# Where two weight matrices are split, and in which order the first tile is normalized, in a fused attention and MLP kernel

## The chip, the cores and the metric
The kernel runs on one core of a Trainium2 chip. The metric is the device time of one execution in microseconds, as the median of several runs. In this kernel TensorE (PE) does the matrix products, VectorE (DVE) and ScalarE (ACT) work on elements and can read the accumulation banks (PSUM), GpSimd (POOL) works on elements in on-chip memory (SBUF), and the queue of SyncE (SP) issues most of the transfers to and from device memory, ACT's queue the others.

## What is computed
With 2048 rows of 1024 elements, 32 heads of 32 and an MLP of width 3584, all in float32:

```
xn  = layernorm(x)
qkv = xn @ wqkv                                  # q, k, v for 32 heads
p   = softmax(q k^T / sqrt(32));  s = concat(p v) @ wo
h   = xn @ w1 + b1
y   = (h * tanh(softplus(h))) @ w2               # mish
out = x + s * silu(y)
```

## The kernel before
Products that need float32 accuracy are made from split operands. A float32 tensor becomes a high part, rounded to the matmul's reduced float32 type (F32R), and a low part, the remainder. Three matmuls (high by high, high by low, low by high; `THREE`) replace one. `copy` makes a high part on ACT, `low(eng, ...)` subtracts on the engine given. So each weight tile must be loaded, split by a copy and a subtract, and then used at once or stored split in device memory and loaded again later. The lists `w1s` and `w2s` hold 28 split tiles each; a W1 tile has 128 columns of W1 (1024x128), a W2 tile 128 rows of W2 (128x1024, in two halves of 512 columns).

The program has five parts.

1. **Prologue.** The first tiles of x (128 rows each) and the four V weight tiles are loaded. `ln_a` takes a tile's statistics (DVE), `ln_r` makes the reciprocal root (two activations), `ln_b` refines it (four 128x1 operations on DVE), `ln_x` normalizes (ACT, for the first two tiles one half on DVE), `ln_t` transposes (PE), and `ln_c` splits the transposed tile into `xc` (ACT copies, DVE subtracts). `v_split` splits a V weight tile `vw`; for the first tile both steps are on POOL, for the last the subtracts are.
2. **V.** Two passes (heads 0 to 15, then 16 to 31) over 16 row tiles. `v_group(i, t)` makes 24 matmuls for one tile; `evac` copies the bank to `vst` and stores it. Pass 0 also transposes the next tile inside each group. The loop index t of pass 0 runs two ahead of the tile that is multiplied. The split `xc` of the last three row chunks (512 rows each) is stored to `xs` by 12 moves, one an iteration from t = 8, two behind the loop. `w1_early` is one step of a pipeline over the first 16 W1 tiles (`W1_V`): store the tile two before, load this one, split the one before (POOL, `w1p` tiles, two buffers). It is called in the last four iterations of pass 0 and in every iteration of pass 1.
3. **QK.** 16 column tiles of the Q and K weights by four row chunks, 24 matmuls each (`qk_group`). `qk_split(f)` splits a weight tile into a buffer of the same two-buffer ring as `w1p`. The result is split into `qst` (two buffers) and stored by ACT's queue. Beside it, `presplit` takes the other 12 W1 tiles and all 28 W2 tiles, half a tile a job (load `praw`; two ticks later copy and subtract on POOL; at the next tick store `pw`), one job a group and two in some. From f = 12 on, head 0's scores are formed to find the maximum of each row (`s_mm`, DVE reductions); for each group of four row tiles, `m_tail` negates the maxima (r1), splits them into an `hl` buffer (r2, ACT and DVE), turns them by a small matmul `mtp` (r3, line 535) and writes them as two rows of the query stack (r4). The steps are placed by ticks of `later`; one tick is one `qk_group`.
4. **Attention and MLP together.** A planner (`Plan`) walks five streams with a cost for each operation and fixes the order on all engines when the program is built: scores for the maxima (`s`), transposed scores (`t`) with the exponentials `p` on ACT, the running sum `z` of the exponentials on POOL (one 128x2048 addition a key tile), products with V (`pv`), and the MLP's `h` and `y` for four row chunks. The MLP takes W1 tiles from `w1s` (ring `w1`, 2 buffers) and W2 halves from `w2s` (`w2_op`, ring `w2`, 5 buffers). `m_chain` is the same maximum chain for the later heads, with a ring `hl` of two.
5. **Output projection** and the final combination.

The lines that place the early W1 steps and the end of V:

```python
        if t > NT - 3:
            w1_early()
...
for t in range(NT):
    v_group(1, t)()
    w1_early()
    if t == 9:
        qk_load(0)
    if t == 12:
        qk_split(0)
        qk_load(1)
```

Of the kernel before, what the change touches and what calls it, by code (L numbers as in the profile page):

```python
# [9 lines left out]
F32 = mybir.dt.float32  # L10
# [15 lines left out]

W1_V = 16
NS = H * NT
# [185 lines left out]
def body(ctx: ExitStack, tc: tile.TileContext, x, wqkv, wo, w1, b1, w2, out):  # L214
# [30 lines left out]
    nc.vector.memset(ones, 1.0)  # L245
    ident = consts.tile([P, P], F32, name="ident")
    make_identity(nc, ident)

    ident_r = consts.tile([P, P], F32R, name="ident_r")
    nc.vector.tensor_copy(ident_r, ident)  # L250
    nc.scalar.preload_act_table_set("natural_log_exp_and_others")
# [18 lines left out]
    def copy(out_, in_, scale=1.0):  # L270
        nc.scalar.activation(out_, in_, AF.Copy, scale=scale)  # L271

    def move(out_, in_, eng=None):

        (eng or nc.sync).dma_start(out_.bitcast(F32), in_.bitcast(F32))

    def low(eng, out_, in_, high):

        eng.tensor_tensor(out_, in_, high.bitcast(F32), ALU.subtract)  # L279
# [17 lines left out]
    xc = [xc0] + [[big.tile([P, 2, HK, 512], F32R, name=f"xc{c}_{i}") for i in range(2)] for c in range(1, NC)]  # L297

    va = ExitStack()
    vp = pool(va, "vp", 2, side="right")  # L300
# [8 lines left out]

    def v_split(i, j, high, rest):  # L310
        raw = vraw.pop((i, j))
        vw[i, j] = w = vp.tile([P, 2, 2, 512], F32R, tag="w", name=f"vw{i}_{j}", bufs=5)
        for k in range(2):
            if high is nc.scalar:
                copy(w[:, 0, k], raw[:, k])
            else:
                high.tensor_copy(w[:, 0, k], raw[:, k])
            low(rest, w[:, 1, k], raw[:, k], w[:, 0, k])

# [72 lines left out]

    def ln_c(t):
        c, r = t // 4, slice(t % 4 * P, t % 4 * P + P)
        for g in range(2):
# [32 lines left out]

    ln_a(0)
# [12 lines left out]
    ln_x(1, True)  # L444
    ln_a(2)
    ln_r(2)
    xts[3] = x_load(3)
    for t in range(2, NT + 2):
        if t < NT:
            ln_b(t)  # L450
        evac = v_group(0, t - 2, 18 if t == 2 else 8, (lambda: ln_t(t - 1)) if t <= NT else None)
        if t <= NT:
            ln_c(t - 1)
        if t < NT:
            ln_x(t)
        for m in (4, 5, 6) if t == 2 else (t + 4,):
            if m < NT:
                xts[m] = x_load(m)
        if t == 2:
            ln_a(3)  # L460
        if t + 2 < NT:
            ln_a(t + 2)
        if t + 1 < NT:
            ln_r(t + 1)
        if t in (NT - 4, NT - 3):
            for j in range(2):
                v_load(1, 2 * (t - NT + 4) + j)
        if t == NT - 2:
            v_split(1, 0, nc.scalar, nc.vector)
        if t == NT + 1:  # L470
            for j in range(1, 4):
                v_split(1, j, nc.scalar, nc.vector)
        evac()
        if t > 7:
            c, k = t // 4 - 1, t % 4 * 2
            move(xs[c][:, :, k:k + 2], xc[c][k // HK][:, :, k % HK:k % HK + 2])
        if t > NT - 3:
            w1_early()
    for k in (4, 6):
        move(xs[NC - 1][:, :, k:k + 2], xc[NC - 1][1][:, :, k % HK:k % HK + 2])  # L480
    nc.sync.dma_start(bias1, b1.rearrange("(f p) -> p f", p=P))
# [41 lines left out]

    hls = [early.tile([P, P], F32R, name=f"hl{i}") for i in range(2)]
    for t in hls:
        nc.vector.memset(t.bitcast(F32), 0.0)

    nc.vector.memset(early.tile([P, 32], F32, name="pad2"), 0.0)
    vt = {}

    def parts(i, n):
        return hls[i][:, :2 * n].rearrange("p (a b) -> p a b", a=2)

    def turn(tp, i):
        nc.tensor.matmul(tp[:, :P], hls[i], ident_r, start=True, stop=True)

# [29 lines left out]
    def m_tail(h, g, mx):  # L566
        nm = early.tile([P, NT], F32, tag=f"nm{g % 2}", name=f"nm{h}_{g}")[:, :4]
        hl = parts(g % 2, 4)
        mt = sp.tile([8, P], F32R, tag="mt", name=f"mt{h}_{g}")

        def r1():
            nc.vector.tensor_reduce(nm, mx[:, :4], axis=AX.X, op=ALU.max, negate=True)

        def r2():
            copy(hl[:, 0], nm)
            low(nc.vector, hl[:, 1], nm, hl[:, 0])

        def r3():
            tp = ps1.tile([P, 512], F32, tag="ps", name=f"mtp{h}_{g}")
            turn(tp, g % 2)  # L580
# [12 lines left out]
    def load_w1(n):  # L593
# [78 lines left out]
    for name, n in (("b", 7), ("s", S_B), ("t", T_B), ("d", D_B), ("o", 1), ("p", PS), ("z", 1), ("e", 1), ("r", 1), ("on", 1),  # L672
                    ("act", ACTS), ("w1", 2), ("w2", W2S), ("xc0", 1), ("xc1", 1), ("v", 2), ("mx", 2), ("nm", 2), ("hl", 2),
                    ("mt", 1), ("h", 2)):
        plan.ring(name, n)
# [47 lines left out]
    def m_chain(h, first, n, maxes, tiles):  # L723
# [5 lines left out]
        def r2(at):  # L729
            tiles["hl"] = at["hl"]  # L730
            copy(parts(tiles["hl"], n)[:, 0], tiles["nm"])

        def r3(at):
            hl = parts(tiles["hl"], n)
            low(nc.vector if h == 0 else nc.gpsimd, hl[:, 1], tiles["nm"], hl[:, 0])

        def r4(at):
            tiles["tp"] = tp = bank(at, f"mtp{h}_{first}")
            turn(tp, tiles["hl"])

# [157 lines left out]

    acts, act_ops, w2t, w2_ops, w1_ops, xc_ops, ys_ops = {}, {}, {}, {}, {}, {}, {}
    tile_time = total / (NC * FT - 1.5)  # L900
# [6 lines left out]

    def w2_op(m, need=()):
        def emit(at):
            w2t[m] = mlp.tile([P, 2, 512], F32R, tag=f"w2{at['w2']}", name=f"w2_{m}")  # L910
            B, dh, j = m // (2 * YB), m // YB % 2, m % YB
            move(w2t[m], w2s[B * YB % FT + j][:, :, dh * 512:(dh + 1) * 512])
        w2_ops[m] = op("SP", 0.1, emit=emit, need=need, take=["w2"], bytes_=P * 1024 * 4)

# [38 lines left out]
    def mish(n, made, t):  # L953
# [54 lines left out]
        act_ops[n] = op("DVE", 0.69, need=[p5], emit=d7, give=[("d", t["own"]), ("b", t["own"]), "h"])  # L1008

    yacc = mlp.tile([P, 4, D], F32, name="yacc")  # L1010

    def y_stream():
        for m in range(W2S):
            w2_op(m, [m_there[0, 3]])
        for B in range(NC * FT // YB):
            c, b = divmod(B, FT // YB)
            done = []
            for dh in range(2):
                for s in range(4):
                    t = {}  # L1020
                    for j in range(YB):
                        n, m_ = YB * B + j, (B * 2 + dh) * YB + j
                        for i, (p, q) in enumerate(THREE):
# [5 lines left out]
                            g = dh * 4 + s + (3 * j + i + 1) / (3 * YB)  # L1029
                            give = (["w2"] if s == 3 and i == 2 else []) + (["act"] if s == 3 and dh and i == 2 else [])  # L1030
# [3 lines left out]
                            m = Op("PE", MM, key=tile_time * due, emit=mm,  # L1034
                                   need=[act_ops[n], w2_ops[m_]], take=["d", "b"] if j == 0 and i == 0 else [], give=give)
                            if j == 0 and i == 0:
# [246 lines left out]
```

## Time and profile before
| | |
|---|---|
| median of 3 runs | 3427.31 us (3425.34 to 3428.84) |
| the profiled execution's own time | 3423.3 us |
| span of its instructions | 3421.1 us |
| busy share of the span: PE, DVE, ACT, POOL | 99%, 68%, 57%, 72% |
| mean granted clock of PE | 0.999 |

The profile comes from one execution. Times are in microseconds from the start of its span. A row of the timeline gives start, duration, engine and line, operation, output<-input, count, and in brackets the idle time before it with what ended it. PE is the matmuls, PEld the weight loads, SPq and ACTq the issuing of transfers. Windows give busy time by engine (with instruction counts), PE's granted clock, the share of DMA time and GB/s. Matmuls overlap, so a busy PE says that it had work, not that it ran at its peak.

### The profile page before, as it was taken

How to read it: one execution, taken by the hardware profiler on the slowest of the kernel's cores; microseconds unless marked ns; L12 is line 12 of the kernel's file. 1: busy time of each engine (PE TensorE's matmuls, PEld its weight loads, DVE VectorE, ACT ScalarE, POOL GpSimd, SP SyncE). 2: the span in 40 equal slices, each digit the busy share in tenths (PEclk: the TensorE clock that was granted, in tenths of full speed). 3: DMA queues.
4: the chain of work that ended last, by engine and by line, in shares of the span. 5: the costliest groups of instructions: out<-in, count | busy, mean ns of one | idle time of the engine just before them, and what ended most of it. 6: DMA issues, size and time to landing. Idle time of an engine off the chain costs nothing.

```text
span 3421.1 us, 45658 instructions
## 1 busy us (share of the span) xinstructions
PE 3389.4 (99%) x17059; PEld 2492.7 (73%) x17059; DVE 2340.5 (68%) x3763; ACT 1942.2 (57%) x3086; POOL 2453.3 (72%) x752
## 2 busy tenths in 40 slices
PE   8999999999999999999999999999999999999999
PEld 7878877677777767777677777777777767777687
DVE  6211226877878777788878787878878788776533
ACT  5211112766666667666666676666666666666621
POOL 0444443988888888888888888888888888888700
PEclk9999999999999999999999999999999999999999
DMA  5989888433334354343434443333445443333482
GB/s 200 326 292 317 301 309 289 124 109 102 118 106 124 102 170 132 116 112 111 124 99 124 149 148 111 112 113 110 124 112 183 123 123 112 112 114 121 136 297 85
DMA packets 289184, 529.60 MB, mean 155 GB/s; under 512 B 88426, under 2 KB 134506, under 8 KB 265706
## 3 DMA queue, kind: packets, MB, share of 16 engines
q1 hardware_dynamic: 269108, 484.74, 46.0%
q10 hardware_dynamic: 19856, 41.95, 3.3%
q8 instruction: 135, 2.21, 0.3%
q14 instruction: 85, 0.70, 0.1%
HBM read 386.89 MB, written 138.67 MB: 154 GB/s over the span
## 4 chain that ended last, share of the span: by engine, by line
PE 87%; DMA 7%; POOL 3%; DVE 2%; SPq 1%; ACT 0%; issue 0%; POOLq 0%; ACTq 0%; DVEq 0%
PE y L1027 18%; PE h L938 17%; PE t L790 13%; PE pv L837 13%; PE s L707 13%; PE op L1124 5%; DMA w2s<-pw 3%; PE v L328 3%; PE qk L631 3%; DMA w1s<-pw 2%; POOL pw L279 1%; DMA w1e<-in_B_w_dram 1%; PE zp L863 1%; DVE mx L713 1%; POOL pw L619 1%; POOL w1p L279 0%
## 5 line engine op out<-in xcount | busy, mean ns | idle before, releaser
L819 POOL TENSOR_TENSOR z<-z,p 128x2048 f32<-128x2048 f32 x448 | 2066.5, 4613 | 192.1 <-ACT p L268 162.5
L268 ACT ACTIVATE p<-t,zero 128x512 f32<-128x512 f32 x2048 | 1384.4, 690 | 636.1 <-PE t L790 618.3
L713 DVE TENSOR_REDUCE mx<-s 128x1 f32<-128x512 f32 x1984 | 1329.6, 686 | 435.4 <-PE s L707 427.8
L1027 PE MATMUL y<-w,act 128*128 128x512 f32 x2688 | 937.4, 391 | 0.6 <-DVE yacc L1047 0.5
L790 PE MATMUL t<-qstack,kstack 128*128 128x512 f32 x2048 | 801.5, 393 | 0.3 <-ACT p L268 0.2
L707 PE MATMUL s<-kstack,qstack 128*128 128x512 f32 x1984 | 779.6, 394 | 3.9 <-DVE mx L713 3.4
L938 PE MATMUL h<-xr,w 128*128 128x512 f32 x2016 | 713.5, 391 | 2.1 <-DMA w<-w1s 2.1
L1027 PEld LDWEIGHTS y<-w,act 128*128 128x128 f32 x2688 | 502.9, 188 | 118.4 <-issue 8.4
L790 PEld LDWEIGHTS t<-qstack,kstack 128*128 128x128 f32 x2048 | 384.0, 188 | 109.0 <-issue 16.8
L707 PEld LDWEIGHTS s<-kstack,qstack 128*128 128x128 f32 x1984 | 371.3, 188 | 126.5 <-issue 24.3
L837 PE MATMUL pv<-p,v 128*32 128x512 f32 x4096 | 459.4, 594 | 0.0
L938 PEld LDWEIGHTS h<-xr,w 128*128 128x128 f32 x2016 | 377.7, 188 | 85.1 <-issue 5.0
L631 PE MATMUL qk<-xc,qkw 128*128 128x512 f32 x1536 | 352.6, 390 | 6.1 <-ACT qkw L271 6.0
L631 PEld LDWEIGHTS qk<-xc,qkw 128*128 128x128 f32 x1536 | 288.9, 188 | 67.3 <-ACT qkw L271 6.4
L837 PEld LDWEIGHTS pv<-p,v 128*32 128x32 f32 x4096 | 123.3, 110 | 282.7 <-issue 282.0
L819 POOL TENSOR_TENSOR z<-p,p 128x2048 f32<-128x2048 f32 x32 | 147.9, 4623 | 243.3 <-ACT p L268 162.3
L1047 DVE TENSOR_TENSOR yacc<-yacc,y 128x512 f32<-128x512 f32 x416 | 283.0, 680 | 52.2 <-PE y L1027 51.4
L938 PE MATMUL h<-xc,w 128*128 128x512 f32 x672 | 242.3, 391 | 0.1
L279 DVE TENSOR_TENSOR qst<-qk,qst 128x512 fp32r<-128x512 f32 x64 | 44.2, 691 | 253.6 <-ACT qst L271 253.6
L271 ACT ACTIVATE qst<-qk 128x512 fp32r<-128x512 f32 x64 | 38.3, 598 | 308.6 <-PE qk L631 235.5
L619 POOL CAST pw<-praw 128x512 fp32r<-128x512 f32 x80 | 50.9, 637 | 195.7 <-DMA w2s<-pw 125.2
L328 PE MATMUL v<-vw,xc 128*128 128x512 f32 x768 | 181.1, 395 | 0.2 <-DVE xc L279 0.2
(93 smaller groups left out, 2366.5 us busy)
## 6 DMA issues: line engine op xcount, KB each, us to landing
w<-w1s SPq DMA_DIRECT2D x112, 1024.0 KB
w<-w2s SPq DMA_DIRECT2D x224, 512.0 KB
w2s<-pw SPq DMA_DIRECT2D x56, 512.0 KB
qstack<-qs SPq DMA_DIRECT2D x96, 256.0 KB
kstack<-ks SPq DMA_DIRECT2D x96, 256.0 KB
praw<-in_B_w_dram SPq DMA_DIRECT2D x80, 256.0 KB
x<-in_A_x_dram SPq DMA_DIRECT2D x32, 512.0 KB
w1s<-w1p SPq DMA_DIRECT2D x16, 1024.0 KB
```

Source lines behind the costliest of these rows:

```text
L268: nc.scalar.activation(out_, in_, fn, bias=zero if bias is None else bias, scale=scale)
L328: nc.tensor.matmul(ps, xc[t // 4][k // HK][:, a, k % HK, (t % 4) * P:(t % 4 + 1) * P], vw[i, k // 2][:, b, k % 2], start=n == 0, stop=n == ...
L631: nc.tensor.matmul(ps, w[:, a, k], xc[c][k // HK][:, b, k % HK], start=n == 0, stop=n == 3 * KT - 1)
L707: nc.tensor.matmul(sp_, qst[h % 3][:, qt * P:(qt + 1) * P], kst[h % 3][:, kc * 512:(kc + 1) * 512], start=True, stop=True)
L713: nc.vector.reduce_max(tiles["mx"][:, qt, kc:kc + 1], tiles[qt, kc], axis=AX.X)
L790: nc.tensor.matmul(tp, kst[h % 3][:, kt * P:(kt + 1) * P], qst[h % 3][:, c * 512:(c + 1) * 512], start=True, stop=True)
L819: nc.gpsimd.tensor_tensor(zs[h], pts[T - 1] if kt == 1 else zs[h], pts[T], ALU.add)
L837: nc.tensor.matmul(pv[h][c * DH:(c + 1) * DH, :], vt[h][:, k, :], pts[T - kt + k][:, c * 512:(c + 1) * 512], start=k == 0, stop=k == NT - 1)
L938: nc.tensor.matmul(t["h"], w1t[n][:, a, k], xts_[c][k // HK][:, b, k % HK], start=i == 0, stop=i == 3 * KT - 1)
L1027: nc.tensor.matmul(t["y"], acts[n][:, p, s * P:(s + 1) * P], w2t[m_][:, q], start=j == 0 and i == 0, stop=j == YB - 1 and i == 2)
L1047: nc.vector.tensor_tensor(ya, ya, t["y"], ALU.add)
L1124: nc.tensor.matmul(ps[t, dh], ohl[t // 4, k][:, a, s * P:(s + 1) * P], wt[k][:, b, r], start=k == 0 and i == 0, stop=k == KT - 1 and i == 2)
```

## The change
- `W1_V` is 12: twelve W1 tiles go through the V stage. `w1_early` is called at t = 5, 8, 11, 14, 17 of pass 0 and at two of three iterations of pass 1. The `xs` stores are spread over every second iteration, from t = 8 of pass 0 to t = 13 of pass 1. x tiles are loaded three ahead instead of four. `qk_split(0)` moves from t = 12 to t = 13.
- `presplit` handles the other 16 W1 tiles and only the first 16 W2 tiles (`W2_Q`): 64 jobs, one a group.
- The last 12 W2 tiles are split where chunk 0 of the MLP first reads them: `w2_op` loads a raw half (one `w2r` buffer), ACT copies it into the `w2` tile, POOL subtracts, and the split half is stored for the other chunks. The `w2` buffer comes free when both the store and the last y matmul are done (`w2_done`).
- The prologue's steps are written one by one. All high parts of the V weights are made on ACT; POOL keeps only the two subtracts of one tile; the pause for the second tile's transposes comes after 21 matmuls instead of 18.
- One `hl` buffer instead of two; r2 of `m_tail` moves from tick 2 to tick 7. One identity tile instead of two.

```diff
-W1_V = 16
+W1_V = 12
+W2_Q = 16
...
-    v_split(0, 0, nc.gpsimd, nc.gpsimd)
+    v_high(0, 0)
     ln_x(0, True)
+    v_low(0, 0, nc.vector)
+    v_high(0, 1)
     ln_t(0)
+    v_low(0, 1, nc.vector)
     ln_c(0)
-    v_split(0, 1, nc.scalar, nc.vector)
+    for k in (2, 3):
+        v_high(0, k)
+        v_low(0, k, nc.vector)
     ln_a(1)
-    v_split(0, 2, nc.scalar, nc.vector)
+    for k in (4, 5):
+        v_high(0, k)
+        v_low(0, k, nc.gpsimd)
+    v_high(0, 6)
+    v_high(0, 7)
+    v_low(0, 6, nc.vector)
     ln_r(1)
     ln_b(1)
-    v_split(0, 3, nc.scalar, nc.gpsimd)
     ln_x(1, True)
+    v_low(0, 7, nc.vector)
...
-        evac = v_group(0, t - 2, 18 if t == 2 else 8, ...)
+        evac = v_group(0, t - 2, 21 if t == 2 else 8, ...)
...
-        for m in (4, 5, 6) if t == 2 else (t + 4,):
+        for m in (4, 5) if t == 2 else (t + 3,):
...
-        if t > 7:
-            c, k = t // 4 - 1, t % 4 * 2
-            move(xs[c][:, :, k:k + 2], ...)
-        if t > NT - 3:
+        if t > 7 and t % 2 == 0:
+            x_store()
+        if t % 3 == 2 and t > 2:
             w1_early()
...
         v_group(1, t)()
-        w1_early()
-        if t == 9:
+        if t % 3:
+            w1_early()
+        if t % 2 and t < 14:
+            x_store()
+        if t == 8:
             qk_load(0)
-        if t == 12:
+        if t == 13:
             qk_split(0)
             qk_load(1)
...
-        for t, fn in ((1, r1), (2, r2), (9, r3), (10, r4)):
+        for t, fn in ((1, r1), (7, r2), (9, r3), (10, r4)):
...
-                [(2, f, half) for f in range(FT) for half in range(2)])
+                [(2, f, half) for f in range(W2_Q) for half in range(2)])
...
             presplit()
-            if f % 2 and f < 14 and c < 3:
-                presplit()
...
     def w2_op(m, need=()):
...
+        if B * YB >= FT or f < W2_Q:
+            w2_ops[m] = w2_took[m] = op("SP", 0.1, emit=emit, need=need, take=["w2"], ...)
+            w2_uses[m] = 1
+            return
...
+        a = op("SP", 0.1, emit=raw, need=need, take=["w2r"], bytes_=P * 512 * 4)
+        w2_took[m] = a = op("ACT", 0.6, need=[a], emit=high, take=["w2"])
+        w2_uses[m] = 2
+        w2_ops[m] = a = op("POOL", 1.3, need=[a], emit=rest, give=["w2r"], key=-1)
+        op("SP", 0.1, emit=lambda at: move(w2s[f][:, :, r], w2t[m]), need=[a], ...,
+           then=lambda o: w2_done(m, o))
```

More of the change, by code (lines that the diff above doesn't have):

```diff
@@ L297, in body @@
     xc = [xc0] + [[big.tile([P, 2, HK, 512], F32R, name=f"xc{c}_{i}") for i in range(2)] for c in range(1, NC)]
+    ident_ = big.tile([P, P], F32, name="ident")
+    make_identity(nc, ident_)
+    nc.vector.tensor_copy(ident_r, ident_)
     va = ExitStack()
@@ L308, in v_load, with v_high, v_low, v_split @@
                           .rearrange("(k p) f -> p k f", p=P))
[L310 to L318, printed above, removed]
+    def v_high(i, k):
+        j, k = divmod(k, 2)
+        if k == 0:
+            vw[i, j] = vp.tile([P, 2, 2, 512], F32R, tag="w", name=f"vw{i}_{j}", bufs=5)
+        copy(vw[i, j][:, 0, k], vraw[i, j][:, k])
+    def v_low(i, k, eng):
+        j, k = divmod(k, 2)
+        low(eng, vw[i, j][:, 1, k], vraw[i, j][:, k], vw[i, j][:, 0, k])
+    def v_split(i, j):
+        for k in (2 * j, 2 * j + 1):
+            v_high(i, k)
+            v_low(i, k, nc.vector)
     def v_group(i, t, cut=0, between=None):
@@ L391, in ln_t, with ln_c @@
                 nc.tensor.transpose(pt[:, k * P:(k + 1) * P], xt[:, (4 * g + k) * P:(4 * g + k + 1) * P], ident)
-    def ln_c(t):
+    def ln_c(t, groups=range(2)):
         c, r = t // 4, slice(t % 4 * P, t % 4 * P + P)
-        for g in range(2):
+        for g in groups:
             p4 = pts_.pop((t, g)).rearrange("p (k n) -> p k n", k=4)
@@ L427, in w1_early, with x_store @@
             split_w(w, raw, True)
+    x_stores = iter([(c, k) for c in range(1, NC) for k in range(0, KT, 2)])
+    def x_store():
+        c, k = next(x_stores)
+        move(xs[c][:, :, k:k + 2], xc[c][k // HK][:, :, k % HK:k % HK + 2])
     ln_a(0)
@@ L522, in body, with parts, turn @@
     stacks(early, 1)
-    hls = [early.tile([P, P], F32R, name=f"hl{i}") for i in range(2)]
-    for t in hls:
-        nc.vector.memset(t.bitcast(F32), 0.0)
+    hl_ = early.tile([P, P], F32R, name="hl")
+    nc.vector.memset(hl_.bitcast(F32), 0.0)
     nc.vector.memset(early.tile([P, 32], F32, name="pad2"), 0.0)
     vt = {}
[L531 to L535, printed above, removed]
+    def parts(n):
+        return hl_[:, :2 * n].rearrange("p (a b) -> p a b", a=2)
+    def turn(tp):
+        nc.tensor.matmul(tp[:, :P], hl_, ident_r, start=True, stop=True)
     def load_head(h, parts=range(3)):
@@ L579, in r3 @@
             tp = ps1.tile([P, 512], F32, tag="ps", name=f"mtp{h}_{g}")
-            turn(tp, g % 2)
+            turn(tp)
             copy(mt, tp[:8, :P])
@@ L729, in r2 @@
         def r2(at):
-            tiles["hl"] = at["hl"]
-            copy(parts(tiles["hl"], n)[:, 0], tiles["nm"])
+            copy(parts(n)[:, 0], tiles["nm"])
         def r3(at):
-            hl = parts(tiles["hl"], n)
+            hl = parts(n)
             low(nc.vector if h == 0 else nc.gpsimd, hl[:, 1], tiles["nm"], hl[:, 0])
@@ L738, in r4 @@
             tiles["tp"] = tp = bank(at, f"mtp{h}_{first}")
-            turn(tp, tiles["hl"])
+            turn(tp)
         def r5(at):
@@ L908, in w2_op, with tile_, raw, high @@
     def w2_op(m, need=()):
+        B, dh, j = m // (2 * YB), m // YB % 2, m % YB
+        f, r = B * YB % FT + j, slice(dh * 512, dh * 512 + 512)
+        def tile_(at):
+            w2t[m] = mlp.tile([P, 2, 512], F32R, tag=f"w2{at['w2']}", name=f"w2_{m}")
         def emit(at):
[L910 to L913, printed above, removed]
+            tile_(at)
+            move(w2t[m], w2s[f][:, :, r])
+        if B * YB >= FT or f < W2_Q:
+            w2_ops[m] = w2_took[m] = op("SP", 0.1, emit=emit, need=need, take=["w2"], bytes_=P * 1024 * 4)
+            w2_uses[m] = 1
+            return
+        def raw(at):
+            w2r[m] = mlp.tile([P, 512], F32, tag="w2r", name=f"w2r_{m}")
+            nc.sync.dma_start(w2r[m], w2[f * P:(f + 1) * P, r])
+        def high(at):
+            tile_(at)
+            copy(w2t[m][:, 0], w2r[m])
+        def rest(at):
+            low(nc.gpsimd, w2t[m][:, 1], w2r[m], w2t[m][:, 0])
+        a = op("SP", 0.1, emit=raw, need=need, take=["w2r"], bytes_=P * 512 * 4)
+        w2_took[m] = a = op("ACT", 0.6, need=[a], emit=high, take=["w2"])
+        w2_uses[m] = 2
+        w2_ops[m] = a = op("POOL", 1.3, need=[a], emit=rest, give=["w2r"], key=-1)
+        op("SP", 0.1, emit=lambda at: move(w2s[f][:, :, r], w2t[m]), need=[a], bytes_=P * 1024 * 4,
+           then=lambda o: w2_done(m, o))
+    def w2_done(m, by):
+        w2_ends.setdefault(m, []).append(by.end)
+        if len(w2_ends[m]) == w2_uses[m]:
+            plan.give("w2", max(w2_ends[m]), by=w2_took[m])
     def xc_op(c):
@@ L1034, in y_stream @@
                             m = Op("PE", MM, key=tile_time * due, emit=mm,
-                                   need=[act_ops[n], w2_ops[m_]], take=["d", "b"] if j == 0 and i == 0 else [], give=give)
+                                   need=[act_ops[n], w2_ops[m_]], take=["d", "b"] if j == 0 and i == 0 else [], give=give,
+                                   then=then)
                             if j == 0 and i == 0:
```

23 lines of the change are left out of this document (10 added, 13 removed).

## The prediction
> **What bounds the kernel now.** I read the page's busy times first, then what TensorE (PE) waited for.
>
> ```profile
> PE 3389.4 (99%) x17059; PEld 2492.7 (73%) x17059; DVE 2340.5 (68%) x3763; ACT 1942.2 (57%) x3086; POOL 2453.3 (72%) x752
> ```
> ```profile
> core 0 of [0], span 3421.1 us
> engine line waited for: us in total, times, longest us
> PE pt L391 <- ACT x L268: 11.9, 2, 9.4
> PE qk L631 <- ACT qkw L271: 6.0, 1, 6.0
> PE s L707 <- DVE mx L713: 3.4, 5, 1.9
> PE h L938 <- DMA w<-w1s: 2.1, 1, 2.1
> PE s L558 <- DVE mx L562: 1.5, 1, 1.5
> ```
> PE is idle for 3421.1 − 3389.4 = 31.7 us, and no matmul is added or removed. So the change can win only from these few waits, and it can lose by making new ones. I take the program in order of time.
>
> **V to QK: the 6.0 us wait.** Windows around it (busy time of each engine, granted clock, DMA share, GB/s), the clock alone, and the chain of waits:
>
> ```profile
> 25.00:110.00 85.00, 85.00 (x433) 71.49 (x432) 46.27 (x133) 45.39 (x83) 1.03 (x2) 1.00 0.66 224
> 110.00:204.00 94.00, 94.00 (x416) 77.83 (x415) 6.95 (x7) 12.44 (x21) 54.25 (x57) 1.00 1.01 332
> 204.00:211.00 7.00, 1.05 (x5) 0.58 (x4) 0.23 (x1) 0.89 (x2) 5.91 (x8) 0.70 0.58 222
> ```
> ```profile
> 206.90:210.30 3.40, 0.00 (x0) 0.00 (x0) 0.00 (x0) 0.19 (x1) 3.16 (x4) 0.50 0.75 310
> 210.30:213.70 3.40, 2.90 (x7) 2.28 (x8) 2.44 (x3) 2.42 (x5) 2.33 (x2) 0.51 0.08 16
> ```
> ```profile
> 206.22 3.82 DMA w1s<-w1p
> ...
> 210.80 28.84 PE qk L631 x120
> ```
> ```profile
> 515.23 5.44 PE qk L631 x24
> ```
> The 16 early W1 tiles begin late (nothing on POOL until 110) and then fill the DMA engines (share 1.01). qk_split(0) needs a w1 buffer whose store lands only at 206.22 + 3.82 = 210.04, and PE waits 7.00 − 1.05 = 5.95 us. In the change the tiles begin at t = 5, in DMA time that was 0.66 used. V's second half then holds 7 loads of 0.52 MB, 9 stores of 1.05, 7 x stores of 1.05, 16 V stores of 0.26 and 2 qk loads of 0.52: 25.7 MB in 16 × 5.44 = 87 us, 295 GB/s where 332 has been reached. The store that qk_split(0) needs is issued behind t = 11, with four groups (22 us) left. The wait goes: **−5.95**. Next late is nothing that I find: weights are split two groups ahead.
> The wait also cost clock: it was at 0.50 from 206.9 to 213.7, and 120 qk matmuls took 28.84 where five groups at 5.44 take 27.2. That is 1.6 with the last one's drain, 1.5 without: **−1.5**.
>
> **QK.** Two waits late in the stage, and what stood before them:
>
> ```profile
> 400.00:500.00 100.00, 98.44 (x433) 80.94 (x432) 23.25 (x36) 14.56 (x25) 44.67 (x48) 1.00 0.90 305
> 500.00:585.00 85.00, 82.54 (x361) 67.01 (x360) 48.43 (x84) 12.75 (x28) 29.45 (x31) 1.00 0.86 287
> ```
> ```profile
> 487.49 0.50 PE L558 MATMUL s<-kstack,qstack 128*128 128x512 f32 x1 [1.47 <-DVE mx L562]
> ...
> 504.92 1.29 POOL L279 TENSOR_TENSOR pw<-praw,pw 128x512 fp32r<-128x512 f32 x1
> ...
> 506.01 0.60 ACT L271 ACTIVATE qst<-qk 128x512 fp32r<-128x512 f32 x1 [8.22 <-DMA w2s<-pw]
> ...
> 507.39 1.10 PE L558 MATMUL s<-kstack,qstack 128*128 128x512 f32 x2 [0.42 <-DVE qst L279]
> ```
> The qk eviction waits 8.22 us for a buffer whose store is stuck among presplit traffic; then DVE's maxima and PE are late. PE lost 1.47 and about 0.6 here. The change has 64 presplit jobs for 80, so 16 × 0.79 = 12.6 MB less of some 108 (80 jobs of 0.79, 64 result stores and 16 weight tiles of 0.52, 3.7 for two heads). But they run to the last group, so load_head(1) now meets them. Bounds: −2.1 to +1.5; I take **−2.1**, as traffic falls by 12% just where the wait is.
>
> **Prologue.** DVE's rows beside POOL's, and the same forms with POOL idle:
>
> ```profile
> 6.45 1.26 POOL L279 TENSOR_TENSOR vw<-vraw,vw 128x512 fp32r<-128x512 f32 x1
> 6.61 1.12 DVE L372 SCALAR_TENSOR_TENSOR tmp<-rs,var 128x1 f32<-128x1 f32 x1 [0.69 <-ACT rs L268]
> ...
> 8.51 1.40 DVE L384 TENSOR_SCALAR x<-x,rs,tmp 128x512 f32<-128x512 f32 x1
> ...
> 13.83 1.28 DVE L359 BATCH_NORM_STATS2 st<-x 128x6 f32<-128x512 f32 x2
> ...
> 22.22 0.22 DVE L372 SCALAR_TENSOR_TENSOR tmp<-rs,var 128x1 f32<-128x1 f32 x1 [0.69 <-ACT rs L268]
> ...
> 23.67 1.66 PE v L328 x6
> ```
> ```profile
> 17.12 0.99 DVE L374 TENSOR_TENSOR rs<-rs,tmp 128x1 f32<-128x1 f32 x1
> 18.14 1.18 DVE L375 SCALAR_TENSOR_TENSOR tmp<-mv,rs 128x1 f32<-128x1 f32 x1
> 19.36 0.55 DVE L384 TENSOR_SCALAR x<-x,rs,tmp 128x512 f32<-128x512 f32 x1
> ```
> A 128x1 operation takes 0.22 alone and 1.12 beside POOL. With POOL's first split gone, tile 0 is normalized from 7.4 instead of 8.51. DVE then has six subtracts of 0.64 to 0.69 with about 1 us of waiting for PE's transposes (to 12.9), statistics 1.28 + 0.4 for their two small steps (14.6), a subtract held by POOL's one remaining split until about 15.4, 0.64 for it and 0.75 for the small chain: tile 1 is normalized at 16.8 instead of 19.36. To tile 1's first subtract come 0.55 + 0.64 + 1.7 + 0.6 + 0.75 + 0.64 more: 21.7. There PE resumes for good (before: 23.67). Less 0.3 for semaphores: **−1.7**. One thing the trace does not show: statistics beside POOL. Held like the small operations they would cost 1.6 more and leave −0.1; not held, −1.7. I take the latter, since 13.83's row reads one tensor; the held rows read two, or are L384, which alone needs 0.55 for 512 elements where the statistics need 0.64.
> The Trainium skill (SBUF — State Buffer, "SBUF: two separate sides") says that DVE and GpSimd share a port pair as an exclusive lock, taken by DVE only in a two-port mode or with two SBUF inputs. By it the statistics run on: the −1.7 end.
>
> **QK to MLP: a new wait.** PE, then DVE, at the boundary:
>
> ```profile
> 578.67 0.33 PE L535 MATMUL mtp<-ident_r,hl 128*128 128x128 f32 x2
> ...
> 582.53 0.51 PE L707 MATMUL s<-kstack,qstack 128*128 128x512 f32 x1 [1.86 <-DVE mx L713]
> ...
> 583.68 0.62 PE L790 MATMUL t<-qstack,kstack 128*128 128x512 f32 x2
> ```
> ```profile
> 579.20 2.48 DVE L562 TENSOR_REDUCE mx<-s 128x1 f32<-128x512 f32 x4
> 581.71 0.17 DVE L727 TENSOR_REDUCE nm<-mx 128x4 f32<-128x16 f32 x1
> 581.80 0.68 DVE L713 TENSOR_REDUCE mx<-s 128x1 f32<-128x512 f32 x1
> 582.39 0.15 DVE L279 TENSOR_TENSOR hl<-nm,hl 128x4 fp32r<-128x4 f32 x1
> ```
> With one hl buffer, the third group's r2 moves from tick 2 to tick 7, so in the changed order its hl subtract stands behind the last four maxima: 581.7 + 0.15. PE's second mtp of 578.67 now waits for it until about 582.0, and s, h and t stand behind it. Six matmuls later (1.4 us) PE is at 583.4 where it was at 582.53: +0.9. It finds its maxima there, so the 1.86 wait is replaced, not added to. The second t needs the row DMA of that mtp, issued near 582.6 to 583.1 and landing near 585.2; PE would be there at 584.7, and was at 583.9: in all **+1.4** (+0.9 to +2.5).
> The idle is now 3.1 us in one piece. At 204.85 the clock was halved 2.05 us after the last matmul, and the idles of 1.47 and 1.86 left it at 1.00 (windows 400 to 585). If it counts by fixed stretches of the 3.4 us that the two 0.50 rows suggest, 3.1 us puts over 2 into one of them in 7 of 10 positions. One stretch at half rate is 1.7, about 0.2 of it under the row's DMA: **+1.5**.
> The Trainium skill (TensorE: Matmul & The Clock Gate, "Why this matters for your kernels") warns of idle gaps over about 3 us, as one window of idle brings the half clock back. Read strictly (a whole idle window of 3.4 us), there is no +1.5 here; the 2.05 above speaks against that reading.
>
> **MLP chunk 0.** Twelve W2 tiles are split here, 24 halves:
>
> ```profile
> 960.00:1280.00 320.00, 319.16 (x1664) 224.24 (x1664) 253.53 (x406) 209.94 (x331) 264.39 (x62) 1.00 0.43 127
> ```
> ```profile
> 800.00:1200.00 400.00, 121.90 (x311) 58.39 (x312) 210.58 (x312) 1.00 0.39 113
> ```
> POOL gets 24 × 1.29 = 31 us where 320 − 264 = 56 are free; ACT 24 × 0.60 = 14 where 110 are free. The second row is t alone: 311 matmuls in 400 us, so a key tile takes 5.1 to 5.4 us. In the changed order each half's subtract stands at least four key tiles ahead of its first y, some 17 us after POOL's own lag: y does not wait. The one raw buffer is the tight place: ACT's copy of the next half follows POOL's subtract by as little as 4 us, and a load takes about 3. ACT is in order, so a late load holds the exps behind the copy, and PE has two t banks. Nothing in the trace shows such a wait: 0 to 0.5 us for each half, 0 to 12; I take **+0.5**, since most distances are 8 us or more. SP's 24 added stores and loads stand ahead of w1 loads with a tile time (24 us) of room.
> PE's order outside key tiles 80 to 140 is unchanged, so the tail's waits (the 2.1 for w1s) stay: 0.
>
> **Sum.** −5.95 − 1.5 − 2.1 − 1.7 + 1.4 + 1.5 + 0.5 = −7.85. The profiled execution took 3423.3, so 3415.4; the median of the runs is 4.0 above it: **3419.5**, 0.23% faster.
>
> **Rivals.** (1) The clock does not fall at the boundary: −9.35, 3418.0. For it: the idle of 1.86 cost no clock, and 3.1 us can fall across two stretches. Chance 0.20. (So it would also be by the strict reading of the Trainium skill's page TensorE: Matmul & The Clock Gate.) (2) QK's waits stay, or statistics are held by POOL: −7.85 + 2.1 to 3.7, about 3422.4. For it: presplits now run beside load_head(1). 0.16. (3) V's chain is late again and the change does not do what it says: 295 against 332 GB/s leaves 11%; about 6 of the 7.45 come back: 3425.5. Against it: 22 us of room. 0.08. (4) Slower: ACT held at raw loads in chunk 0. At 0.9 us a half this is 24 × 0.9 − 0.5 = +21, 3440.6; from 0.35 a half the gain is gone, from 0.64 it is slower by over 0.2%. 0.06. My forecast has 0.50; its own range is 3417 to 3422.5.
>
> **Numbers.** 0.2% (6.9 us) is about what a measurement can tell from no change, so faster means below 3420.5: 0.65 of the forecast, 0.9 of (1), 0.1 of (2): 0.52. Slower is (4): 0.06. Same: 0.42. The range 3415.0 to 3426.5 takes in (1) to (3) and the prologue's and boundary's bounds.
>
> **What would show it.** PE at qk's start without a wait and at clock 1.00; no waits of s L558 late in QK; PE resuming near 21.7; a wait of about 3.1 us at the second mtp, with the clock row behind it; ACT's w2 copies without a wait for their loads. I am wrong if V's windows still show a DMA share near 1.0 to the end, or if t waits for ACT between 960 and 1280.

## The result and the profile after
The changed kernel's median is 3413.88 us (3412.52 to 3420.35, 6 runs), the one before 3427.85 us (3425.34 to 3428.84, 6 runs) on the same chip: 0.9963 of the time, 95% interval 0.9950 to 0.9976. The forecast was 3419.5, faster; the median lies 1.1 us under the low end of its range (3415.0 to 3426.5). The profiled execution took 3414.67 us (before: 3423.3).

The page of the changed kernel, busy times by engine, and its list of PE's waits (total, times, longest):

```profile
span 3412.9 us, 45611 instructions
...
PE 3389.4 (99%) x17059; PEld 2493.5 (73%) x17059; DVE 2337.6 (68%) x3764; ACT 1955.3 (57%) x3112; POOL 2431.8 (71%) x724
```
```profile
PE pt L400 <- ACT x L268: 9.0, 2, 8.4
PE mtp L560 <- DVE hl L279: 2.9, 1, 2.9
PE v L337 <- ACT xc L271: 1.3, 1, 1.3
PE h L993 <- ACT p L268: 1.2, 1, 1.2
PE s L730 <- DVE mx L736: 1.1, 3, 0.5
PE h L993 <- DMA xr<-xs: 0.8, 1, 0.8
PE t L812 <- ACT p L268: 0.5, 1, 0.5
```
PE's busy time is the same 3389.4, so by these records all of the 8.2 us between the spans is PE's idle time; both spans hold about as much half clock (9.2 us before, 8.1 after). The lines of before that stood for V to QK (6.0) and late QK (1.5 and 0.4) are gone. New are the line of `mtp` (2.9), that of v for `xc` (1.3, where pt waits 9.0 instead of 11.9) and that of h for the x rows of the MLP's second chunk (`xr`, 0.8). The windows of V and of the boundary to QK (busy by engine, granted clock, DMA share, GB/s), and the piece of the chain that starts there:

```profile
25.00:110.00 85.00, 85.00 (x428) 71.50 (x427) 44.87 (x128) 44.26 (x80) 11.28 (x12) 1.00 0.69 229
110.00:204.00 94.00, 94.00 (x417) 77.82 (x416) 6.45 (x8) 14.70 (x25) 35.92 (x37) 1.00 0.90 305
204.00:211.00 7.00, 7.00 (x33) 5.79 (x32) 4.32 (x5) 1.82 (x4) 1.32 (x2) 1.00 0.43 120
```
```profile
204.30 266.56 PE qk L656 x1176
```
The DMA share of V's second half is 0.90 where it was 1.01, with 305 GB/s (the forecast had worked out 295). PE goes from V into QK without a wait, at full clock, and 1176 qk matmuls follow as one piece.

The matmuls of both programs come in the same order but for a few stretches, so the start of the same matmul tells where the 8.2 us came from:

| matmul | before | after | difference |
|---|---|---|---|
| V, the 101st | 43.30 | 42.75 | −0.55 |
| first of QK | 210.80 | 204.14 | −6.66 |
| QK, the 24th (still so at the 1001st) | 217.47 | 209.35 | −8.12 |
| QK, the 1301st (still so at the last early s) | 515.97 | 504.24 | −11.73 |
| t, the 21st | 602.57 | 593.56 | −9.01 |
| t, the 401st | 1090.30 | 1082.82 | −7.48 |
| t, the 601st | 1349.72 | 1340.35 | −9.37 |
| y, the 2001st | 2629.32 | 2620.75 | −8.57 |
| output projection, the 101st | 3265.07 | 3256.85 | −8.22 |

### The profile page after: what moved, and what is told of

It is laid out like the page before. It is cut to its first block, busy times and chain, and to the rows that moved or that the text cites. A ratio compares the mean times of both kernels' runs of the same rounds, so it can differ in the third digit from the quotient of the medians.

```text
span 3412.9 us, 45611 instructions
## 1 busy us (share of the span) xinstructions
PE 3389.4 (99%) x17059; PEld 2493.5 (73%) x17059; DVE 2337.6 (68%) x3764; ACT 1955.3 (57%) x3112; POOL 2431.8 (71%) x724
## 4 chain that ended last, share of the span: by engine, by line
PE 97%; DVE 1%; DMA 1%; ACT 1%; issue 0%; SPq 0%; POOL 0%; ACTq 0%; DVEq 0%
PE y L1083 18%; PE h L993 18%; PE t L812 13%; PE s L730 13%; PE pv L859 13%; PE qk L656 10%; PE op L1182 5%; PE v L337 5%; PE zp L885 1%; DVE mx L736 1%; PE pt L400 0%; ACT p L268 0%; PE s L583 0%; DMA xr<-xs 0%; DMA w2r<-in_B_w_dram 0%
## 5 line engine op out<-in xcount | busy, mean ns | idle before, releaser
L644 POOL CAST pw<-praw 128x512 fp32r<-128x512 f32 x64 | 39.5, 618 | 232.4 <-DMA w1s<-pw 123.7
```

## The experiments
All edits are to the changed kernel unless said. Theory: each term of the forecast's sum has the cause that the forecast gave it. Rival causes stand with each run. "Changed" is the changed kernel; its 11 runs (6 and, below, 5) have a median of 3413.1.

### The V stage: number of early tiles, or bytes late in the stage
```diff
-W1_V = 12
+W1_V = 16
-        if t % 3 == 2 and t > 2:      # pass 0
+        if t > NT - 3:
             w1_early()
-        if t % 3:                     # pass 1
-            w1_early()
+        w1_early()
```


> The changed kernel with the early W1 tiles of the V stage as before: 16 of them, begun in the last four groups of V's first half, one for each group of the second. Stores of the x chunks, loads of the first qk weights and everything else stay as changed; QK then has 56 presplit jobs. Theory (tiles begun late fill the DMA engines to the end of V and the store that the first qk weights need lands late): a wait of 4 to 7 us ahead of the first qk matmul, and half clock behind it, plus 5.5 to 8.5 us: 3419 to 3422 for the median. Rival (the spread stores of x, or the other order of loads, did it): the wait is under 2 us and the time within 2.5 us of the changed kernel's.

Measured: 3422.29 us (3420.70 to 3427.45, 11 runs), 8.4 over the changed kernel's first median. Waits and windows of this run:

```profile
PE qk L655 <- ACT qkw L271: 7.1, 1, 7.1
```
```profile
110.00:204.00 94.00, 94.00 (x416) 77.84 (x415) 4.84 (x6) 13.03 (x22) 53.67 (x57) 1.00 1.01 352
...
211.00:214.00 3.00, 2.49 (x6) 1.96 (x7) 2.03 (x3) 1.95 (x4) 0.00 (x0) 0.50 0.98 397
```
The DMA engines are full to the end (1.01), the wait of 7.1 is back, half clock behind it. The spread of the x stores, kept here, did not prevent it. The second run keeps 16 tiles but starts them early:

```diff
-W1_V = 12
+W1_V = 16
-        if t % 3 == 2 and t > 2:      # pass 0
+        if t % 2 and t > 2:
             w1_early()
```


> The changed kernel with 16 early W1 tiles as before, but spread: eight steps in V's first half (every odd group from 3), ten in its second, as the changed kernel has there. QK then has 56 presplit jobs. Theory (what counts is how many bytes V's second half must move, not how many tiles there are): no wait ahead of the first qk matmul (under 0.3 us), time within 1.5 us of the changed kernel's, 3412.5 to 3415.5. Rival (the smaller number of tiles is what helped): a wait of 3 us or more there, 3417 or more.

Measured: 3413.39 us (3411.35 to 3419.84, 5 runs), no wait at the first qk matmul, and:

```profile
110.00:204.00 94.00, 94.00 (x416) 77.84 (x415) 8.71 (x9) 15.30 (x26) 40.43 (x41) 1.00 0.93 317
204.00:211.00 7.00, 7.00 (x33) 5.79 (x32) 5.12 (x7) 1.64 (x3) 1.83 (x2) 1.00 0.63 238
```
So 16 tiles do no harm if they begin early; what counts is how much the second half must move. At 305 and 317 GB/s the store arrives in time, at a share of 1.01 it does not. Twelve tiles begun late were not run, and neither was the early start without the spread of the x stores.

### QK: the number of presplit jobs
```diff
-W2_Q = 16
+W2_Q = 24
             presplit()
+            if f % 2 and f < 14 and c < 3:
+                presplit()
```


> The changed kernel with 24 of W2's tiles split in QK, not 16, and with the second presplit job that the kernel before had in three groups of every odd weight tile up to 13: 80 jobs as before. Four W2 tiles are left for the MLP's first chunk. V stays as changed. Theory (the qk eviction waited for its store among presplit traffic, and DVE's maxima behind it): TensorE's waits late in QK come back, 1.4 to 2.6 us of idle that cost 2.9 to 3.6 us, as every matmul right behind a wait starts 0.1 to 0.4 us later too: 3416 to 3418. Rival (they came from V's lateness, or from a stretch at half clock, not from the number of jobs): no such wait, 3413 to 3414.5.

Measured: 3417.56 us (3415.08 to 3423.74, 11 runs), plus 3.7, which is a net figure: the edit also takes 16 halves out of the MLP's first chunk. Late in QK, PE and then ACT:

```profile
476.71 0.51 PE L583 MATMUL s<-kstack,qstack 128*128 128x512 f32 x1 [0.70 <-DVE qst L279]
478.86 0.49 PE L583 MATMUL s<-kstack,qstack 128*128 128x512 f32 x1 [1.65 <-DVE mx L587]
479.46 2.83 PE L656 MATMUL qk<-xc,qkw 128*128 128x512 f32 x11
```
```profile
475.33 0.60 ACT L271 ACTIVATE qst<-qk 128x512 fp32r<-128x512 f32 x1 [5.76 <-DMA ks<-qst]
```
It is the chain of before: an eviction held for a buffer until a store lands (5.76), then DVE, then PE. The idle is 2.35, but the same matmuls lie 4.4 us later behind it (up to the last waits 1.65 ahead of the changed profile, then 2.79 behind it). Of this, 3.3 arises at these two waits. The row behind the second shows part of the reason: the matmul right behind the waiting one starts 0.60 later (478.86 to 479.46), where 24 in 5.44 make 0.227 the pace. The other 1.1 comes from four such late starts between 498 and 500, with gaps of at most 0.10 us, too short for the list of waits. A short wait costs more than its idle time.

### The prologue
```diff
-        evac = v_group(0, t - 2, 21 if t == 2 else 8, ...)
+        evac = v_group(0, t - 2, 18 if t == 2 else 8, ...)
```


> The changed kernel with tile 1's transposes behind 18 of the first V group's 24 matmuls, not 21, as the kernel before had it. Nothing else. In the changed kernel TensorE waits 0.66 us ahead of these transposes and 1.31 + 0.22 behind them, and a stretch at half clock follows (22.21 to 25.62), 1.7 us of loss. Theory (fixed stretches): three matmuls (0.68 us) move from ahead of the transposes to behind them, so the idle ahead is 1.34, the idle behind 0.6 to 0.8, and neither lies together in one stretch as before: no half clock near 22, steady V groups 1.7 us earlier than in the changed kernel's profile, about 3413.0 for that profile's 3414.67, and a median lower by 0.5 to 1.7, as its runs may not all have lost the stretch. Rival (the clock counts the idle time of the whole prologue, or the fall there has another cause): the half clock stays, and the time is the same within 0.5 us.

Measured: 3411.91 us (3411.23 to 3417.89, 5 runs); the profiled span is 3410.0. The windows from 18.8 of the changed kernel, of this one, and of the run with 16 early tiles, whose prologue is the changed kernel's:

```profile
18.80:22.20 3.40, 1.88 (x7) 0.91 (x7) 2.54 (x10) 2.70 (x5) 0.00 (x0) 1.00 0.01 2
22.20:25.60 3.40, 3.40 (x14) 2.90 (x13) 3.23 (x10) 1.61 (x5) 0.00 (x0) 0.50 0.00 0
```
```profile
18.80:22.20 3.40, 2.58 (x10) 1.49 (x9) 2.54 (x10) 2.70 (x5) 0.00 (x0) 1.00 0.02 6
22.20:25.60 3.40, 3.40 (x21) 2.88 (x20) 3.22 (x10) 1.88 (x5) 0.00 (x0) 1.00 0.00 0
```
```profile
18.80:22.20 3.40, 1.88 (x7) 0.95 (x6) 2.54 (x10) 2.70 (x5) 0.00 (x0) 1.00 0.01 2
22.20:25.60 3.40, 3.40 (x20) 2.87 (x20) 3.19 (x10) 1.90 (x5) 0.00 (x0) 1.00 0.00 0
```
The changed kernel has 14 matmuls in 3.4 us at clock 0.50, the others 20 and 21 at 1.00: 1.65 us for the groups behind. But the third pair has the same 1.88 of work ahead as the first and keeps its clock. So this run cannot show that the edit made the difference: with the unedited prologue 3 of 7 profiles lost this stretch and 4 did not. That points to the position of the stretches (below). None of the four profiles with 18 matmuls lost it, which is too few to tell from chance.

The order of before, put into the changed kernel:

```diff
+    # as before: v_split(0, 0) on GpSimd first, the other splits
+    # behind ln_c(0), ln_a(1) and ln_b(1), 18 matmuls ahead
```


> The changed kernel with the prologue's order as before: the first weight tile's split on GpSimd ahead of all, the later splits where the kernel before had them, 18 matmuls ahead of tile 1's transposes; loads, V stage, QK and MLP as changed. Theory (profiles: the new order brings V's steady groups forward by 2.2 us, of which the changed kernel's own profile lost 1.7 to a stretch at half clock that four other profiles of the same prologue did not have): the wait of 2.5 us ahead of tile 1's transposes is back; V's steady groups begin 2.2 us later than in the profiles without that stretch, or 3.9 with one behind the 2.5 us; the median is 2 to 3.5 us over the changed kernel's 3413.9: 3416 to 3417.5. With the V stage's 8.4 and QK's 3.7 and less the boundary's 2.4 this makes up the 13 to 14 us between the medians. Rival (the prologue gives what the two first profiles show, 0.55): 3414 to 3415, and something else moves the medians.

Measured: 3415.73 us (3414.66 to 3420.30, 5 runs), 1.85 over the changed kernel's first median. Its PE, and the two stretches:

```profile
20.32 1.10 PE L400 MATMUL pt<-ident_r,x 128*128 128x128 f32 x8 [2.59 <-ACT x L268]
```
```profile
18.07:21.48 3.41, 1.16 (x9) 1.13 (x10) 3.27 (x7) 0.81 (x1) 1.33 (x2) 1.00 0.42 145
21.48:24.89 3.41, 3.41 (x10) 2.62 (x9) 2.62 (x9) 2.75 (x5) 0.00 (x0) 0.50 0.01 2
```
The wait of before is back, and here it cost a stretch at half clock, as in neither profile of the kernel before. V's steady groups start 3.1 us later than in the profiles of the new prologue without that stretch, 1.4 later than in the changed kernel's with it. The median lies between the two expectations, just under the 3416 of the theory and above the 3415 of the rival.

### The boundary to attention and MLP
```diff
-        for t, fn in ((1, r1), (7, r2), (9, r3), (10, r4)):
+        for t, fn in ((1, r1), (3, r2), (7, r3), (8, r4)):
```


> The changed kernel with the steps of each group's row of maxima at ticks 1, 3, 7 and 8 in place of 1, 7, 9 and 10: with one buffer, the write at tick 3 of the next group (4 ticks later) comes right behind the read at tick 7 of this one, and the last group's small subtract no longer stands behind the last four maxima. Theory: TensorE's wait of 2.91 us at the second turn of the boundary goes; the 1.9 us wait of the maxima behind it that the kernel before had (1.86) comes back, and the stretch at half clock (571.76 to 575.17) goes in most positions: minus 1.0 for the wait and up to minus 1.7 for the clock, so 3412 to 3413.5 for the profile's 3414.67, median minus 1.0 to minus 2.7. Rival (the last maxima and the row behind them set the pace, the order of the small steps only names the wait): under 0.5 us.

Measured: 3415.34 us (3412.41 to 3416.88, 5 runs): no gain in the time. From the last early s to the 21st t it took 2.6 us less than the changed kernel; the profile lost it again in the tail, where h waited 2.63 for a W1 tile and the output projection 2.02 for DVE, with a stretch at half clock. It was run next together with the 18 matmuls:

> The changed kernel with both edits of the first set of runs: tile 1's transposes behind 18 matmuls, and the steps of the maxima at ticks 1, 3, 7 and 8. Theory (they are independent, and each takes away one stretch at half clock or a wait): no record of half clock ahead of the tail, no 2.9 us wait at the boundary; up to the first MLP chunk 4.0 us ahead of the changed kernel's profile (1.65 and 2.4); the waits of the tail (1.2 to 4.6 us so far) are not touched and may differ: 3408 to 3411.5, median 3410. Rival (the tail gives back what comes earlier, as the profile with the new ticks lost 4.2 us there): 3413 or more.

Measured: 3410.55 us (3410.11 to 3413.55, 5 runs). A second set beside the changed kernel on one chip:

> The changed kernel once more, beside the version with both edits on the same chip. Theory (same prologue, another position of the clock's stretches): waits of 0.66, 1.31 and 0.22 us in the prologue and 2.91 at the boundary as before; the stretch at half clock behind the prologue in about one of three executions; median 3412.5 to 3415. Rival (the first six runs were lucky): median over 3416.

> The version with both edits once more (transposes behind 18 matmuls; steps of the maxima at ticks 1, 3, 7 and 8). Theory: 2.5 to 4 us under the changed kernel on the same chip, median 3409.5 to 3411.5. Rival (the first median was a matter of the tail's waits, which differ from run to run): within 1.5 us of the changed kernel's median.

Measured: 3412.82 (3412.10 to 3417.38, 5 runs) for the changed kernel, 3410.98 (3410.84 to 3412.07, 5 runs) for both edits. The difference of 1.8 misses the 2.5 expected, and of all runs, nine of ten with both edits lie below the fastest of eleven without. PE at the boundary, the changed kernel, then both edits, then the edit of the prologue alone:

```profile
570.07 0.33 PE L560 MATMUL mtp<-ident_r,hl 128*128 128x128 f32 x1 [2.91 <-DVE hl L279]
```
```profile
567.35 0.50 PE L730 MATMUL s<-kstack,qstack 128*128 128x512 f32 x1 [1.65 <-DVE mx L587]
568.54 0.50 PE L730 MATMUL s<-kstack,qstack 128*128 128x512 f32 x1 [0.69 <-DVE mx L587]
```
```profile
568.42 0.33 PE L560 MATMUL mtp<-ident_r,hl 128*128 128x128 f32 x1 [2.91 <-DVE hl L279]
...
572.60 0.47 PE L812 MATMUL t<-qstack,kstack 128*128 128x512 f32 x1 [0.98 <-DMA qstack<-mt]
...
578.04 0.47 PE L812 MATMUL t<-qstack,kstack 128*128 128x512 f32 x1 [0.40 <-DMA qstack<-mt]
```
The last one is what tells most: it has the wait of 2.91 without a half clock behind it, and yet the boundary cost it 2.69 us (against the same matmuls of before), the changed kernel 2.72. Without the half clock, t finds the row's DMA not landed and waits 0.98 and 0.40. The new ticks do not keep the clock in every execution either: in two of the four profiles that have them a stretch at half clock followed these waits, and the boundary gained 1.0 and 1.2 us there, against 2.5 in the other two.

### The MLP's first chunk
```diff
-W2_Q = 16
+W2_Q = 8
```


> The changed kernel with 8 of W2's tiles split in QK, not 16: 20 tiles, 40 halves, are split where the MLP's first chunk reads them, in place of 24 halves, through the same one raw buffer; QK has 48 jobs. Theory (ScalarE and GpSimd have the room, the loads land in time): the first chunk costs no more than 1 us over the changed kernel's, in all 3413 to 3415. Rival (ScalarE is held at the raw loads, and with it the exps): t waits for ScalarE between 880 and 1350 us, 16 halves more at 0.35 to 0.9 us each, plus 6 to 14 us: 3419 to 3428.

Measured: 3416.05 us (3414.07 to 3421.59, 10 runs), plus 2.2: more than the theory, far less than the rival. For 16 more halves that is 0.14 us each, whatever held them. In this run's profile the 21st to the 601st t take 2.3 us more than in the changed kernel's, but t's waits for ACT there are only 0.6; s waited 1.3 for DVE's maxima near 1237, and why was not followed. The changed kernel's raw tile, as its own view has it, then the issue of one load, and ACT at the one place where PE felt it:

```profile
  DMA w2r<-in_B_w_dram: 14.2, 5
```
```profile
1064.73 0.60 SPq L948 DMA_DIRECT2D w2r<-in_B_w_dram  x1
```
```profile
1067.83 0.60 ACT L271 ACTIVATE act<-h 128x512 fp32r<-128x512 f32 x1
1074.31 0.63 ACT L271 ACTIVATE w<-w2r 128x512 fp32r<-128x512 f32 x1 [5.88 <-DMA w2r<-in_B_w_dram]
...
1075.32 0.68 ACT L268 ACTIVATE p<-t,zero 128x512 f32<-128x512 f32 x1
```
ACT stood 5.88 us at a raw load with the exps behind it, and t then waited 0.51. The copy began 9.6 us after its load was issued, where the forecast took a load at about 3. Five copies in 24 were held, 14.2 us in all, and one of them reached PE.

The last run took the edits together, with 16 tiles started early and W2's split at 20 tiles in QK:

> Both edits of the first set (transposes behind 18 matmuls; steps of the maxima at ticks 1, 3, 7 and 8), with 16 early W1 tiles spread as in the run with eight steps in V's first half, and 20 of W2's tiles split in QK, so that 64 presplit jobs stay and eight W2 tiles, not twelve, are left for the MLP's first chunk. Theory: V as without the two more tiles' groups (no wait at the first qk matmul), QK without waits, the first chunk 0 to 1 us shorter than with twelve: 3409 to 3411, beside 3410.6 for both edits alone. Rival (the first chunk's split costs nothing, and the tail's waits decide): the same as both edits within 1 us either way.

Measured: 3411.19 us (3410.95 to 3414.96, 5 runs), no better than both edits alone.

### Why medians and profiles differ
The profiles are 8.6 us apart, the medians 14.0. The kernel before, once more:

> The kernel before, once more, to see which of its waits or clock stretches differ from one execution to the next: its profile was 4.5 us under the median of its runs, the changed kernel's 0.8 over. Theory (the clock is counted in fixed stretches of 3.41 us, and a stretch in which TensorE had work for under about 40% is followed by one at half clock, which costs 1.7 us; where the stretches lie against the program differs from run to run): the new profile has the same waits within 0.3 us (9.4, 2.5, 6.0, 1.5, 1.9 and 2.1), but half-clock records at other places, behind the 2.5 us of idle in the prologue in about 3 of 4 positions and behind the 1.9 us at the boundary in about half; its runs lie 3424 to 3429, in steps of about 1.7 us, median 3427. Rival: one of the waits itself is longer in most executions; then the new profile shows it (6.0 at V to QK become 8 or more, or the QK waits of 1.5 and 0.4 become 4 or more) and the clock records are the same two.

Measured: 3426.27 us (3421.11 to 3430.41, 11 runs), the profiled execution 3423.32. Its waits:

```profile
PE qk L631 <- ACT qkw L271: 4.7, 1, 4.7
...
PE s L558 <- DVE mx L562: 2.1, 1, 2.1
PE h L938 <- DMA w<-w1s: 1.0, 1, 1.0
```
The rival missed: no wait is much longer. But they did move by up to 1.3 us, more than the 0.3 expected, and behind the wait of 2.1 stands a stretch at half clock (489.67 to 493.08) that the first profile did not have. 70 runs of the kernel before have a clock on record:

| mean granted clock | runs | mean time, us |
|---|---|---|
| 0.999 and over | 15 | 3424.6 |
| 0.998 | 33 | 3427.0 |
| 0.997 | 19 | 3429.5 |
| 0.996 | 3 | 3433.1 |

So 0.001 of clock goes with 2.4 to 3.6 us. Both profiled executions belong to the first row: their half-clock records inside the span are 9.2 and 6.8 us long, half of which over 3421 is 0.0013 and 0.0010. The mean of all runs is 0.0021 down, so a typical run loses two such stretches more than the profiles show. At about 2.6 us for 0.001 this is 2.1 to 2.9 of the 3.7 us between profile and median. The changed kernel's profile (0.0012 down) is like its runs (0.0011). What makes up the rest, about 1 us, stays open.

## Why the prediction was right, and where it was not
- **V to QK, −7.45.** Measured −7.57 in the profile (from −0.55 to −8.12), +8.4 in the median when undone. Right, by the bytes of the second half.
- **QK, −2.1.** The waits went, because there are fewer jobs; the rival by which load_head(1) would meet them did not come. The term was mis-sized: −3.61. The step added up idle times (1.47 and 0.6); the price is the delay of the start, with the slow starts behind each wait.
- **Prologue, −1.7.** Tile 1 was normalized at 16.58 (forecast 16.8) and PE resumed at 21.50 (21.7). The disputed price fell as taken: beside POOL two statistics took 1.28, as without it, while a two-input subtract took 1.40, about twice as long as elsewhere. DVE and PE, then POOL:

```profile
12.80 1.28 DVE L368 BATCH_NORM_STATS2 st<-x 128x6 f32<-128x512 f32 x2
...
14.44 1.40 DVE L279 TENSOR_TENSOR vw<-vraw,vw 128x512 fp32r<-128x512 f32 x1
...
16.58 0.55 DVE L393 TENSOR_SCALAR x<-x,rs,tmp 128x512 f32<-128x512 f32 x1
...
21.50 2.35 PE L337 MATMUL v<-vw,xc 128*128 128x512 f32 x6 [0.22 <-DVE xc L279]
```
```profile
12.60 2.69 POOL L279 TENSOR_TENSOR vw<-vraw,vw 128x512 fp32r<-128x512 f32 x2 [11.29 <-ACT vw L271]
```
  That the statistics ran on and the subtract was held agrees with the Trainium skill (SBUF — State Buffer, "SBUF: two separate sides"). The gain, 2.2 us in the profiles that kept the clock, was cut to 0.55 in this one by a stretch at half clock that the sum did not have; undoing the order costs 1.85 in the median.
- **Boundary, +1.4 and +1.5 for the clock.** The wait of 3.1 measured 2.91, and the clock fell, as forecast. The total measured 2.72 for 2.9. But the two do not add: where the clock held, the row's DMA took its place (2.69). In that profile the first term was a little over its high end of 2.5, and the second adds about 0. So rival (1), minus 1.5, was wrong as a price though its condition did occur. The strict reading of the Trainium skill (TensorE: Matmul & The Clock Gate, "Why this matters for your kernels": a whole idle window) is not what the runs show; 2.91 us of idle halved the clock in seven of the eight profiles that have this wait.
- **Chunk 0, +0.5.** The subtracts did stand far enough ahead for y, which gained no wait. But ACT's copies did wait for loads, whose absence was listed as a sign of being right, and t waited 0.51 for ACT, which was listed as a sign of being wrong: the load that was taken at about 3 us took up to 9.6. The wait of h for `xr` at 1244 (0.83) is also new, at a DMA share of 1.04 from 1230 to 1245. The sum had nothing for it, and its cause was not tested. Even so, from the 21st t to the 601st the change is −0.36. Four short waits of before between 1252 and 1258 us (0.84 in all) went, and the rest was not followed. In the other profiles with the same split it lies between −0.65 and −1.4. Rival (4) had the mechanism, once in 24 halves; its price for a half was 0.9, and each further half measured 0.14, other waits included.
- **Tail, 0.** From the 601st t to the last s, 1.1 us came back in steps under 0.1 us that I did not follow. The tail itself came out even: h's wait is 0.87 shorter, and the wait of `zp` (the matmuls that add z up over the partitions) with slower starts behind it took 0.86. But these waits differ by up to 2 us from profile to profile (0.6 to 2.6 for h).
- **The absolute time.** The sum (−7.85) was right to 0.8 us of the profiles' −8.6, in part by luck: QK gave 1.5 more than its term and the first chunk 0.9 more, the prologue 1.15 less, and 1.1 came back further on. The step that failed is the last: "the median of the runs is 4.0 above" its profile held for the kernel before only. The changed kernel's median is 0.8 under its profile. A likely reason is that the waits that went were occasions on which many runs, though not the profiled one, lost clock as well; the second profile of the kernel before did so late in QK, and the run with the old prologue did at its wait of 2.59. That this makes up the whole offset is not shown.

## What to carry over
Price a wait by the start of the matmuls behind it, not by its idle time, and ask what is late next: here a stretch at half clock and a wait for a DMA behind the same gap cost as much as the second alone. Before adding a profile's sum to a median, see whether the profiled execution is a typical one; the mean granted clock of each run tells it. Where transfers are behind at a stage's end, moving some of them earlier can be enough, without having fewer.

## What was not expected of the hardware
The records of half clock begin and end on a grid of 3.413 us that lies differently in each execution. In all 14 profiles, between the first record of full clock (at 12 to 16 us) and the last 12 us of the span, each of the 13 stretches of that grid with 1.95 us or more of PE idle was followed by one at half clock; of 20 with 1.5 to 1.9 us nine were; with less only one was, which was itself at half clock. So a little over half a stretch of idle, not a whole one, is enough. Three stretches of the grid around the wait of 2.91, in the changed kernel and in the run with the edit of the prologue alone:

```profile
564.93:568.34 3.41, 2.23 (x11) 1.67 (x9) 1.47 (x3) 1.07 (x3) 0.00 (x0) 1.00 0.00 0
568.34:571.75 3.41, 1.68 (x7) 1.34 (x8) 2.70 (x8) 0.36 (x2) 0.00 (x0) 1.00 0.90 332
571.76:575.17 3.41, 3.41 (x11) 2.65 (x10) 1.88 (x3) 1.64 (x4) 0.00 (x0) 0.50 0.94 217
```
```profile
563.82:567.23 3.41, 1.69 (x9) 1.20 (x7) 2.02 (x4) 1.07 (x3) 0.00 (x0) 1.00 0.12 44
567.24:570.65 3.41, 2.23 (x10) 1.82 (x11) 2.67 (x8) 0.84 (x3) 0.00 (x0) 1.00 0.81 301
570.66:574.06 3.40, 2.42 (x10) 1.69 (x10) 2.07 (x4) 1.72 (x4) 0.00 (x0) 1.00 0.97 216
```
The changed kernel had its 2.91 us as 1.18 and 1.73 and lost a stretch; the prologue edit had 1.73 and 1.18 and did not. The grid cuts the same gap differently in each execution, and with that the clock went or stayed. But the larger piece was 1.73 in both, so the idle time of one stretch alone does not order the cases between 1.5 and 1.9, and what does is open. That the grid runs by itself is also what the Trainium skill says (TensorE: Matmul & The Clock Gate, "Part 1: The HAM clock gate").
